# Block-sparse attention and a squared-relu layer on one core: PSUM banks oldest first, later landing times, and score visits of two slots in part of the third batch

## The chip, the cores and the metric

The kernel runs on one core of a Trainium2 chip. The metric is the time of one execution on the device in microseconds (us); a kernel is described by the median of several executions. The profile is of one execution. Its span runs from the first to the last instruction of the program, and the execution's own time is a little longer.

A core has five engines that run side by side, each working through its own instructions in order: TensorE (PE in the profile; its weight loads are listed apart as PEld), VectorE (DVE), ScalarE (ACT), GpSimd (POOL) and SyncE (SP), which here only issues DMAs. Matrix products land in PSUM, an accumulation store of eight banks. ACT and DVE read it from there; POOL works only on SBUF here.

## The reference, cut to what matters

Inputs are q, k and v (4 batches, 8 heads, 768 positions, 64 values), a list of sampled blocks, and two weight matrices. Attention is dense arithmetic under a mask of 32 by 32 blocks, and a two-layer network with a squared relu follows:

```python
scores = scale * np.matmul(q, k.transpose(0, 1, 3, 2))
mask = np.abs(blk_i - blk_j) <= window
mask = mask | (blk_i == 0) | (blk_j == 0) | (blk_i == n_blocks - 1) | (blk_j == n_blocks - 1)
for qb in range(n_blocks):
    for kb in sampled_blocks[qb]:
        mask[qb * block:(qb + 1) * block, kb * block:(kb + 1) * block] = True
scores = np.where(mask, scores, -1000000000.0)
scores = scores - np.max(scores, axis=-1, keepdims=True)
attn = np.exp(scores)
attn = attn / (np.sum(attn, axis=-1, keepdims=True) + 1e-09)
return np.matmul(attn, v).astype(np.float32)
...
x = attn_out.transpose(0, 2, 1, 3).reshape(B * S, H * D)   # 3072 x 512
h = x @ w_in                                               # 512 -> 2048
r = np.maximum(h, 0.0)
g = r * r
return (g @ w_out).astype(np.float32)                      # 2048 -> 512
```

## The kernel before, in words

**Tiling.** Heads are taken in pairs, four pairs to a batch, 16 in all. A *slot* is one piece of attention: a head pair, a tile of queries (128 wide for the first 256 queries of the first batch, 256 wide elsewhere) and two or three chunks of 128 keys. The slots stand in one list, `order`: 40 for the first batch, then 36 for each of the other three. A slot's steps are:

- `scores` (L443): K times Q on TensorE, with the two heads in the two halves of the array's rows, 64 rows each. For the first 256 queries of the first batch the mask is added by a further matmul (L447).
- `exps` (L454): the exponential, on ACT, from PSUM into SBUF (pT).
- `masks` (L461): elsewhere DVE multiplies pT by a mask tile MK of zeros and ones.
- `values` (L483): pT times V on TensorE, with a column of ones that gives the sum; `normalize` (L491, L493) on DVE divides, and the result is transposed into xT, by TensorE in the first batch (L500) and by DMA later (L512).

TensorE does scores in a 64-row mode and nearly everything else in a 128-row mode. The planner charges 0.096 us (`SWITCH`) for a change between them. To change less often, `attend` takes several slots in one *visit*: `GROUPS` says for each batch, and each third of its queries, how many. A 3 stands for all slots of one pair and query tile, which are three.

The dense layers work on tiles of 128, 256 or 384 tokens. `hidden` (L541) makes units of two or four chunks of the 2048 hidden columns, each unit in two or four parts that the planner places one by one; `relu` (L550 on ACT, L552 on DVE) and `square` (L560 on ACT, L562 on POOL) follow, and `output` (L585) accumulates over 16 chunks in bank py. Tokens of one batch pass the dense layers while the next batch is in attention, and the last batch's run alone at the end.

**PSUM.** Two banks serve `po` and `py`. The other six are three tiles X of 1024 columns, two banks each. A slot of scores takes a whole tile (`X2`), as does a unit of hidden columns of a 384-token tile. Transposes, mask tiles and the 512-column hidden units of the first batch take one bank (`X1`). `bank()` chooses: each candidate has a key, the lowest wins.

**Order of the work.** It is computed on the host, before anything runs, by the planner `run_schedule`: it keeps an expected time for each engine and buffer, and each step puts next the task that can start first; ties go by `key` (made uneven by `tie`, from `SEEDS` and `TIES`). The instructions then stand in that order in each engine's queue, held on the chip by semaphores, not by the planner's times. The durations, latencies (`LAT`), `AHEAD` (how much earlier a task of the dense layers must be to go ahead of one of attention with a key under 100), `bias` (a handicap for an engine when a task may go to several), `PACE0` and `PACE` (the earliest time for a batch's scores, by slot), `LEAD` (how long before that the casts of Q and K may start) and `arrive` (when each first-batch input is assumed to have landed) are numbers of the plan alone.

**Loads.** SP issues the first batch's inputs at the start, and ACT two K loads. Later pairs come through `load` on SP, held by `loads_gate`, small DMAs that wait for parts of w_out. POOL issues the weights' DMAs (L417, L420) behind a small copy (L414) that waits for one of the first batch's V loads. Casts (L248 on DVE and POOL, L246 on ACT) and transposes bring Q and K into QK; from the second batch on the transposes are DMAs on SP (L402).

Of the kernel before, what the change touches and what calls it, by code (L numbers as in the profile page):

```python
# [25 lines left out]
def kernel(  # L26
# [21 lines left out]
    HP = H // 2  # L48
# [24 lines left out]


    CB, GATES = 0.4, (6, 7)
    GROUPS = (1, 1, 1), (2, 2, 2), (3, 3, 3), (3, 3, 3)
    QT0, ADDED, ALONE = [(0, 128), (128, 128), (256, 256), (512, 256)], (0, 128), (0, 128)
    MASKED = ((256, 512, 6.5), (512, 768, 8.0), (0, 256, 38.0))
    tasks = []
    LAT = {"PE": 0.23, "DVE": 0.06, "ACT": 0.06, "POOL": 0.08, "SP": 1.4}  # L80
    OVER = {"PE": 0.0, "DVE": 0.08, "ACT": 0.09, "POOL": 0.03, "SP": 0.0}
    SWITCH, SHARE, SLACK = 0.096, 0.85, 0.1
    AHEAD = {"PE": 0.043, "DVE": 0.108, "ACT": 0.176, "POOL": 0.0, "SP": 0.0}
    LEAD = 5.943
    HOLD = 0
    PACE0, PACE, SINGLE, MASK_AT = 39.28, 1.726, 1, 17.0

# [1 line left out]
    class Buf:  # L91
        def __init__(self, pool):
# [2 lines left out]

    TIES = 2.583, 1.777
    SEEDS = (
            621053, 621053, 621053, 162164, 486097, 621053, 621053, 88936, 279485,  # L100
            617998, 621925, 997023, 39474, 741514, 621053, 644142, 104467, 983473,
            256392, 272690, 973551, 604649, 254998, 99264)

    def tie(n):
        x = (n + 1) * 2654435761 & 0xFFFFFFFF ^ SEEDS[n // 64] * 2246822519 & 0xFFFFFFFF
# [18 lines left out]
    def run_schedule(free, bufs, dma_free, mode=128):  # L124
# [12 lines left out]
        def bank(pool, now, gone):  # L137
            n = 2 if pool == "X2" else 1
            best = None
            for c in range(0, 6, n):  # L140
                mine = [cells[i] for i in range(c, c + n)]
                if any(i in gone for i in range(c, c + n)) or any(b and b.holds for b in mine):
                    continue
                r = max([now] + [b.free for b in mine if b])
                o = cells[c ^ 1]
                k_ = (round(r, 4), n == 1 and not (o and o.holds), c)
                if best is None or k_ < best[0]:
                    best = (k_, c, r)
            return best
# [448 lines left out]
    def T_(engs, key, f, *args, **kw):  # L598
        return Task(engs, key, (lambda e: f(*args, e)), **kw)
# [1 line left out]


    arrive = {(0, 1, 0): 3.4, (0, 0, 0): 4.2, (0, 1, CP): 4.55, (1, 0, 0): 5.7, (1, 1, 0): 6.7, (2, 0, 0): 7.2, (2, 1, 0): 8.3, (0, 2, 0): 9.4,
              (3, 0, 0): 9.8, (3, 1, 0): 10.9, (1, 2, 0): 12.4, (2, 2, 0): 13.5, (3, 2, 0): 14.6}
    arrive.update({(u, 0, 2): (15.5, 16.2, 16.8, 17.5)[u] for u in range(HP)})

    KEYS_OF = {P: [tuple(range(CP)), tuple(range(CP, NCH))], QW: [(2 * c, 2 * c + 1) for c in range(CP)]}
    OPEN = [(0, 0), (0, 1), (1, 0), (2, 0), (1, 1), (3, 0), (2, 1), (3, 1)]
# [56 lines left out]
    def attend(group, add):  # L665
        s = min(order.index(a) for a in group)
        bufs = {a: Buf("X2") for a in group}
        area = sum(a[2] * len(a[3]) for a in group) / 512
        deps = [ev[a[0]][1, n] for a in group for n in a[3]]
        deps += [ev[a[0]][0, n] for a in group for n in range(a[1] // P, (a[1] + a[2]) // P)]  # L670
        sc = T_(("PE", (0.44 if add else 0.22) * area), s, scores, group, add, bufs,
                deps=deps + (mr[:1 + (group[-1][1] + group[-1][2] > QW)] if add else []) + sc_all[-1:], get=[bufs[a] for a in group], mode=64,
                after=PACE0 + PACE * (s - N0) * (1.06 - 0.0006 * (s - N0)) if s >= N0 else 0.0, paced=group[0][1] >= QW or s >= N0)
        sc_all.append(sc)
        for i, a in enumerate(group):
            u, q0, w, cs = a
            sc_of[u].append(sc)
            s = order.index(a)
            part = w * len(cs) / 512
            pt = Buf("pT")  # L680
            ex = T_(("ACT", 0.2 + 0.82 * part), s, exps, a, deps=[sc], lead=sc.engs["PE"] * (len(group) - 1 - i) / len(group), get=[pt], put=[bufs[a]])
            if not add:
                ex = T_(("DVE", 0.68), s - 1, masks, a, deps=[ex] + [mk[n, c] for n in cs for c in range(q0, q0 + w, P)], port=True)
            if cs[0] == 0:
                ob[u, q0] = Buf(po_pool(u, q0))
            va = T_(("PE", 0.245 * part), s + 2.023, values, a, deps=[ex] + cv[u] + va_all[-1:] + (kws if po_pool(u, q0) == "y" else []),
                    get=[] if cs[0] else [ob[u, q0]], put=[pt], mode=128)
            va_all.append(va)
            va_of[u].append(va)
            if cs[-1] == NCH - 1:  # L690
                b, a_ = divmod(u, HP)
                by_dma = b > 0
                xqb = Buf("xq")
                nm = T_(("DVE", 0.3 + 0.16 * w / P), s - 9, normalize, u, q0, w, deps=[va], get=[xqb], put=[ob[u, q0]] if by_dma else [])
                kw = {}
                if b not in xb:
                    xb[b] = Buf("xT")
                    kw = dict(get=[xb[b]])
                if by_dma:
                    mu[u, q0] = T_(("SP", 1.22), s - 9, x_transp_dma, u, q0, w, deps=[nm], put=[xqb], dma=0.6, **kw)  # L700
                    continue
                xt = T_(("PE", 0.06 * w / P), s - 9, x_transp, u, q0, w, deps=[nm], put=[xqb], mode=128)
                mu[u, q0] = T_({"DVE": 0.11 + 0.09 * w / P, "ACT": 0.2 + 0.09 * w / P}, s - 9, x_evac, u, q0, w, deps=[xt], put=[ob[u, q0]], **kw)
# [10 lines left out]
    kws = []  # L714
# [28 lines left out]
    for k_, T in enumerate(TILES + [None]):  # L743
        hs = [(T, f) for f in range(0, NF, per_unit(T))] if T else []
        ys = [(TILES[k_ - 1], i, part) for i in range(len(y_tiles(TILES[k_ - 1]))) for part in range(NY)] if k_ else []
        both = [((i + 0.5) / len(hs), 0, x) for i, x in enumerate(hs)]
        both += [((i + 0.5) / len(ys), 1, x) for i, x in enumerate(ys)]
        for _, kind, x in sorted(both, key=lambda z: z[:2]):
            n_key += 1
            t = x[0]  # L750
            b, c0, w = t
            if kind == 0:
                f = x[1]
                need = [mu[b * HP + a, q0] for a in range(HP) for q0, qw in QT[b] if q0 < c0 + w and c0 < q0 + qw]
                w *= per_unit(t)
                wide = w > 512
                hb, rb = Buf("X2" if wide else "X1"), Buf("r")
                last_use = c0 + t[2] == S and f + per_unit(t) == NF
                parts = 4 if wide else 2
                hd = []  # L760
                for part in range(parts):
                    end = part == parts - 1
                    hd.append(T_(("PE", HID[w] / parts), n_key - (0.6 if part else 0.5), hidden, t, f, part, parts, hb,
                                 deps=hd[-1:] or need + [wl[f * NWP // NF], wl[(f + per_unit(t) - 1) * NWP // NF]],
                                 get=[] if part else [hb], put=[xb[b]] if last_use and end else [], mode=128, yields=not part))
                h1 = hd[-1]
                rr = T_(RELU[w], 200, relu, t, f, deps=[h1], get=[rb], put=[hb], bias={"ACT": 0.092})
                n = 1 if wide else per_unit(t)
                for i in range(0, per_unit(t), n):
                    gb = Buf("g")  # L770
                    gbuf[t, f + i + n - 1] = gb
                    sq = T_(SQ[n * t[2]], n_key, square, t, f, i, n, deps=[rr], get=[gb], put=[rb], bias={"ACT": 0.673})
                    sq_of.update({(t, f + i + j): sq for j in range(n)})
            else:
                _, i, part = x
                ts, cs = y_tiles(t)[i]
                n = (cs[1] - cs[0]) / d_model
                fs = range(part * NF // NY, (part + 1) * NF // NY)
                if part == 0:
                    yb = Buf(y_pool(t, i))  # L780
                last_i = i == len(y_tiles(t)) - 1
                yy = T_(("PE", 0.432 * n), n_key, output, t, i, ts, cs, part, yb,
                        deps=[sq_of[t, f] for f in fs] + [wl[NWP + f * NWP // NF] for f in fs] + ([yprev] if part else []),
                        get=[] if part else [yb], put=[gbuf[t, f] for f in fs if (t, f) in gbuf] if last_i else [], mode=128)
                yprev = yy
                if part == NY - 1:
                    sb = Buf("ys")
                    yc = T_({"ACT": 0.22 + 0.365 * n, "DVE": 0.15 + 0.53 * n}, 150, out_copy, t, i, cs, deps=[yy], get=[sb], put=[yb])
                    T_(("SP", 0.55), 0, store, t, i, ts, cs, deps=[yc], put=[sb], late=2.0, dma=0.7)
# [34 lines left out]
```

## Time and profile before

| | |
|---|---|
| median of 5 executions | 277.69 us (276.65 to 277.8) |
| the profiled execution's own time | 277.8 us |
| its span | 276.0 us |
| TensorE busy | 262.0 us (95%), clock 0.999 |
| ACT busy | 224.6 us (81%) |
| DVE busy | 166.6 us (60%) |
| POOL busy | 86.8 us (31%) |
| DMA, mean over the span | 134 GB/s |

A line of a timeline gives the start, the length, the engine, the line of the kernel, the operation, what it writes and reads, and how many instructions are merged; a bracket at its end is the idle time of the engine just before it, and what ended that. A line of the waits gives who waited for whom, the total in us, how many times, and the longest. Matmuls are pipelined: a group's length includes the last one's way through the array, so the cost of one is read from the distance between starts. Some matmul records are missing from the trace; the weight loads are complete.

### The profile page before, as it was taken

What the parts mean: (1) busy time and instruction counts of PE and PEld (TensorE: products, weight loads), DVE (VectorE), ACT (ScalarE), POOL (GpSimd) and SP (SyncE); (2) the same over time, 40 slices, a digit from 0 to 9 for tenths busy, and PEclk for the clock granted to TensorE, in tenths of its full rate; (3) what the DMA queues carried; (4) which work ended last, traced back from release to release, by engine and by line L of the source; (5) the groups of instructions that cost most, each with busy time, mean ns of one, the idle gap of its engine ahead of it and who ended that gap; (6) DMA issues with size and microseconds to landing.
All of it is one profiled execution on the core that took longest, in us unless ns stands there. A gap on an engine that the chain in (4) does not pass through costs nothing.

```text
span 276.0 us, 7322 instructions
## 1 busy us (share of the span) xinstructions
PE 262.0 (95%) x2992; PEld 166.3 (60%) x3032; DVE 166.6 (60%) x339; ACT 224.6 (81%) x294; POOL 86.8 (31%) x110
## 2 busy tenths in 40 slices
PE   8988999889998999999999999999999999999995
PEld 5776665766566565556656556656565666555544
DVE  7886999743877888666856476685665565011010
ACT  3788999958997999999989999899798998646511
POOL 3192327444621126533131251312221112333210
PEclk9999999999999999999999999999999999999999
DMA  6999999999572229765771123442411011011112
GB/s 195 373 214 201 208 221 334 297 287 354 117 216 57 59 40 208 137 216 139 214 219 21 48 63 67 103 72 60 104 57 43 20 57 50 10 40 39 38 68 84
DMA packets 51881, 36.91 MB, mean 134 GB/s; under 512 B 30984, under 2 KB 48904, under 8 KB 51848
## 3 DMA queue, kind: packets, MB, share of 16 engines
q1 hardware_dynamic: 47080, 31.86, 42.2%
q0 software_dynamic: 4224, 4.19, 9.4%
q8 instruction: 23, 0.38, 0.6%
q10 hardware_dynamic: 544, 0.39, 0.5%
q14 instruction: 10, 0.08, 0.1%
HBM read 27.26 MB, written 6.29 MB: 122 GB/s over the span
## 4 chain that ended last, share of the span: by engine, by line
PE 86%; ACT 4%; DVE 4%; issue 3%; DMA 2%; SPq 1%; ACTq 0%; DVEq 0%
PE X L541 30%; PE py L585 27%; PE X L443 12%; PE po L483 12%; DMA ks<-in_k_dram 2%; PE X L585 2%; ACT pT L454 2%; ACT r L550 2%; DVE pT L461 1%; DVE QK L248 1%; SPq L274 1%; PE X L365 1%; PE X L395 1%; PE po L500 0%; DVE MK L373 0%
## 5 line engine op out<-in xcount | busy, mean ns | idle before, releaser
L454 ACT ACTIVATE pT<-X 128x1024 bf16<-128x1024 f32 (+1 forms) x148 | 138.1, 1008 | 8.8 <-PE X L443 6.1
L461 DVE TENSOR_TENSOR pT<-pT,MK 128x1024 bf16<-128x1024 bf16 x132 | 93.4, 728 | 24.2 <-ACT pT L454 23.4
L562 POOL TENSOR_TENSOR g<-r 128x384 bf16<-128x384 f32 (+1 forms) x65 | 59.3, 914 | 151.2 <-ACT r L550 128.6
L541 PE MATMUL X<-xT,w_in_sb 128*128 128x384 bf16 (+2 forms) x640 | 99.8, 294 | 2.9 <-ACT r L550 2.5
L585 PE MATMUL py<-w_out_sb,g 128*128 128x512 bf16 (+1 forms) x328 | 87.6, 374 | 3.4 <-issue 1.9
L541 PEld LDWEIGHTS <-w_in_sb 128*128 128x128 bf16 x640 | 54.4, 97 | 33.1 <-issue 6.7
L550 ACT ACTIVATE r<-X 128x768 f32<-128x768 f32 (+1 forms) x65 | 48.7, 755 | 22.2 <-PE X L541 19.3
L483 PEld LDWEIGHTS <-pT 128*128 128x128 bf16 x1152 | 47.4, 98 | 17.7 <-issue 4.2
L483 PE MATMUL po<-VT,pT 128*128 128x65 bf16 x1152 | 53.3, 193 | 0.1
L585 PEld LDWEIGHTS <-g 128*128 128x128 bf16 x400 | 34.3, 98 | 27.8 <-issue 4.4
L443 PE MATMUL X<-QK 64*128 64x256 bf16 (+1 forms) x624 | 46.6, 263 | 1.9 <-ACT pT L454 1.1
L443 PEld LDWEIGHTS <-QK 64*128 64x128 bf16 x624 | 25.9, 94 | 20.2 <-issue 15.4
L560 ACT ACTIVATE g<-r 128x384 bf16<-128x384 f32 (+1 forms) x55 | 29.8, 542 | 3.0 <-DVE r L552 1.4
L491 DVE RECIPROCAL rs<-po 128x4 f32<-128x4 f32 (+1 forms) x52 | 9.3, 179 | 35.5 <-PE po L483 35.3
L248 DVE COPY ys<-py 128x512 f32<-128x512 f32 x17 | 11.7, 686 | 27.6 <-PE py L585 27.6
L493 DVE TENSOR_TENSOR xq<-po,rs 128x256 bf16<-128x256 f32 (+1 forms) x52 | 21.0, 404 | 1.8
L248 POOL CAST VT<-vs 128x768 bf16<-128x768 f32 x15 | 15.7, 1044 | 19.2 <-issue 11.2
L248 DVE CAST qc<-ks 128x768 bf16<-128x768 f32 (+1 forms) x15 | 11.3, 753 | 0.8 <-DMA ks<-in_k_dram 0.7
L248 DVE CAST qc<-qs 128x768 bf16<-128x768 f32 (+2 forms) x16 | 9.6, 604 | 0.0
L246 ACT COPY ys<-py 128x512 f32<-128x512 f32 (+1 forms) x6 | 3.3, 558 | 5.5 <-PE py L585 5.3
L447 PE MATMUL X<-R,oh 64*128 64x128 bf16 x96 | 6.7, 216 | 0.0
L585 PE MATMUL X<-w_out_sb,g 128*128 128x512 bf16 (+1 forms) x32 | 6.0, 326 | 0.0
(54 smaller groups left out, 76.3 us busy)
## 6 DMA issues: line engine op xcount, KB each, us to landing
vs<-in_v_dram SPq DMA_DIRECT2D x16, 384.0 KB, 6.7
out_dram<-ys SPq DMA_DIRECT2D x23, 256.0 KB, 2.0
ks<-in_k_dram SPq DMA_DIRECT2D x15, 384.0 KB, 5.0
qs<-in_q_dram SPq DMA_DIRECT2D x12, 384.0 KB, 4.0
w_in_sb<-in_moe_w_in_dram POOLq DMA_DIRECT2D x4, 512.0 KB, 9.7
w_out_sb<-in_moe_w_out_dram POOLq DMA_DIRECT2D x4, 512.0 KB, 16.0
qs<-in_q_dram SPq DMA_DIRECT2D x4, 256.0 KB, 7.7
xT<-xq SPq DMA_TRANSPOSE x36, 2.3
```

What stands on the lines that cost most here:

```text
L248: (V if e == "DVE" else G).tensor_copy(out=out, in_=in_)
L443: nc.tensor.matmul(ps[:, h, j * w:(j + 1) * w], QK[i][hs, 1, ksl], QK[i][hs, 0, qsl], start=j == 0, stop=not add, skip_group_check=True)
L454: A.activation(out=pT[:, :, 0:n], in_=stile.pop(a)[:, :, 0:n], func=AF.Exp, scale=scale)
L461: V.tensor_tensor(out=pT, in0=pT, in1=m[:, None].broadcast_to([P, 2, len(cs), w]), op=AOP.mult)
L483: nc.tensor.matmul(po[:, qc, h, :], pT[:, h, j * w + qc * P:j * w + (qc + 1) * P], VT[i][:, h, n, 0:VW], start=(n == 0 and qc == 0 and h = ...
L491: V.reciprocal(out=rs, in_=po[:, :, :, D:VW])
L493: V.tensor_tensor(out=xq, in0=po[:, :, :, 0:D], in1=rs.broadcast_to([P, n, 2, D]), op=AOP.mult)
L541: nc.tensor.matmul(htile[T, f][:, i], w_in_sb[:, kc, (f + i) * P:(f + i + 1) * P], xT[b][:, kc, c0:c0 + w], start=(kc == 0), stop=(kc == K ...
L550: A.activation(out=to, in_=src, func=AF.Relu)
L560: A.activation(out=g, in_=r, func=AF.Square)
L562: (G if e == "POOL" else V).tensor_mul(out=g, in0=r, in1=r)
L585: nc.tensor.matmul(ytile[T, i], gtile[T, f][:, ts * P:(ts + 1) * P], w_out_sb[:, f, cs[0]:cs[1]], start=(f == 0), stop=(f == NF - 1))
```

## The change

It has these parts:

- `bank()`: a bank's place in the choice is set by the time at which it was freed plus 0.8 us, where that is later than the present time, in place of the time at which it was freed. Whether a partner bank is in use, and the number of the bank, still settle ties.
- `arrive`: the V loads of pairs 1, 2 and 3 are assumed to land at 13.4, 14.5 and 15.4 us (12.4, 13.5, 14.6 before), the last queries at 16.1, 16.7, 17.3 and 17.9 (15.5, 16.2, 16.8, 17.5).
- `GROUPS`: the first two thirds of the third batch's queries are visited in twos rather than threes.
- The planner's numbers: the seeds and sizes of the ties, `AHEAD`, `LEAD`, `PACE0`, `PACE`, the place of `values` behind its scores, and ACT's bias for relu and square.

No instruction of the computation is added or taken away.

```diff
-    GROUPS = (1, 1, 1), (2, 2, 2), (3, 3, 3), (3, 3, 3)
+    GROUPS = (1, 1, 1), (2, 2, 2), (2, 2, 3), (3, 3, 3)
...
-    AHEAD = {"PE": 0.043, "DVE": 0.108, "ACT": 0.176, "POOL": 0.0, "SP": 0.0}
-    LEAD = 5.943
+    AHEAD = {"PE": 0.031, "DVE": 0.078, "ACT": 0.219, "POOL": 0.0, "SP": 0.0}
+    LEAD = 9.606
     HOLD = 0
-    PACE0, PACE, SINGLE, MASK_AT = 39.28, 1.726, 1, 17.0
+    PACE0, PACE, SINGLE, MASK_AT = 41.486, 1.677, 1, 17.0
...
-    TIES = 2.583, 1.777
+    TIES = 1.442, 1.763
     SEEDS = (
-            621053, 621053, 621053, 162164, 486097, 621053, 621053, 88936, 279485,
-            617998, 621925, 997023, 39474, 741514, 621053, 644142, 104467, 983473,
-            256392, 272690, 973551, 604649, 254998, 99264)
+            355681, 98427, 98427, 98427, 857545, 98427, 97069, 50148, 911331,
+            98427, 50466, 222927, 270327, 703620, 362781, 613003, 726090, 53435,
+            690252, 701928, 821263, 803756, 192065, 79588)
...
                 r = max([now] + [b.free for b in mine if b])
                 o = cells[c ^ 1]
-                k_ = (round(r, 4), n == 1 and not (o and o.holds), c)
+                old = max([now] + [b.free + 0.8 for b in mine if b])
+                k_ = (round(old, 4), n == 1 and not (o and o.holds), c)
...
-              (3, 0, 0): 9.8, (3, 1, 0): 10.9, (1, 2, 0): 12.4, (2, 2, 0): 13.5, (3, 2, 0): 14.6}
-    arrive.update({(u, 0, 2): (15.5, 16.2, 16.8, 17.5)[u] for u in range(HP)})
+              (3, 0, 0): 9.8, (3, 1, 0): 10.9, (1, 2, 0): 13.4, (2, 2, 0): 14.5, (3, 2, 0): 15.4}
+    arrive.update({(u, 0, 2): (16.1, 16.7, 17.3, 17.9)[u] for u in range(HP)})
...
-            va = T_(("PE", 0.245 * part), s + 2.023, values, a, deps=[ex] + cv[u] + va_all[-1:] + (kws if po_pool(u, q0) == "y" else []),
+            va = T_(("PE", 0.245 * part), s + 3.182, values, a, deps=[ex] + cv[u] + va_all[-1:] + (kws if po_pool(u, q0) == "y" else []),
...
-                rr = T_(RELU[w], 200, relu, t, f, deps=[h1], get=[rb], put=[hb], bias={"ACT": 0.092})
+                rr = T_(RELU[w], 200, relu, t, f, deps=[h1], get=[rb], put=[hb], bias={"ACT": 0.112})
...
-                    sq = T_(SQ[n * t[2]], n_key, square, t, f, i, n, deps=[rr], get=[gb], put=[rb], bias={"ACT": 0.673})
+                    sq = T_(SQ[n * t[2]], n_key, square, t, f, i, n, deps=[rr], get=[gb], put=[rb], bias={"ACT": 0.721})
```

## The prediction

> **What bounds the kernel now.** I read first the page's busy times and slices: TensorE is the only engine near its limit, and the throttle never took its clock.
>
> ```profile
> PE 262.0 (95%) x2992; PEld 166.3 (60%) x3032; DVE 166.6 (60%) x339; ACT 224.6 (81%) x294; POOL 86.8 (31%) x110
> ```
>
> Busy time hides when the idle 14.0 us fall, so next comes busy time by stage (columns: stretch, length, busy time with instructions of PE, weight loads, DVE, ACT, POOL, clock, DMA share, GB/s). The cuts are mine: opening, rest of the first batch's attention, a stretch without score visits, second batch, third, fourth, and what is left of the dense layers.
>
> ```profile
> 0.00:20.00 20.00, 17.39 (x277) 13.06 (x278) 15.90 (x50) 12.93 (x23) 8.70 (x27) 1.00 0.90 265
> 20.00:50.00 30.00, 27.75 (x467) 19.27 (x470) 25.61 (x60) 28.31 (x37) 11.77 (x12) 1.00 1.12 248
> 50.00:63.00 13.00, 11.20 (x148) 9.10 (x147) 6.52 (x13) 9.53 (x17) 5.12 (x5) 1.00 1.17 282
> 63.00:105.00 42.00, 40.53 (x516) 26.40 (x523) 32.31 (x60) 37.77 (x46) 14.56 (x13) 1.00 0.53 135
> 105.00:165.00 60.00, 58.92 (x646) 35.95 (x654) 40.16 (x72) 55.13 (x70) 21.07 (x24) 1.00 0.53 142
> 165.00:232.00 67.00, 65.69 (x712) 40.09 (x726) 42.32 (x81) 60.77 (x75) 14.86 (x18) 1.00 0.28 62
> 232.00:276.00 44.00, 40.54 (x243) 22.47 (x242) 3.81 (x7) 20.17 (x32) 10.75 (x13) 1.00 0.14 50
> ```
>
> PE's idle time is 2.6, 2.3 and 1.8 us in the first 63 us, 1.5 in the second batch, 1.1 and 1.3 in the two after it, 3.5 in the last (nearly all of it the last copy and store, which nothing here touches). Later on PE is full: work added there lengthens the program, and only waits before about 105 us can be taken away. PE's waits, by who ended them:
>
> ```profile
> PE X L541 <- ACT r L550: 2.5, 4, 0.8
> PE py L585 <- issue: 1.9, 12, 0.2
> PE X L443 <- ACT pT L454: 1.1, 2, 1.0
> PE X L365 <- ACT MK L371: 0.4, 1, 0.4
> PE X L443 <- DVE MK L373: 0.4, 1, 0.4
> ```
>
> The "issue" line is mostly missing records (328 and 32 matmuls of L585 shown beside 400 weight loads), not a wait. What a change of banks can reach is 2.5 + 1.1 = 3.6 us: hidden-layer matmuls waiting for a relu, scores waiting for an exponential. The longest of the first kind, in PE's and ACT's order of time:
>
> ```profile
> 52.19 1.49 PE L541 MATMUL X<-xT,w_in_sb 128*128 128x128 bf16 x20
> 54.49 0.60 PE L541 MATMUL X<-xT,w_in_sb 128*128 128x256 bf16 x4 [0.81 <-ACT r L550]
> ...
> 53.86 0.58 ACT L550 ACTIVATE r<-X 128x512 f32<-128x512 f32 x1
> ```
>
> The 20 matmuls are a unit of 16 and the first half (4) of a 256-wide unit; the wait comes before its second half. That half writes a bank which the unit already holds, so it can't be waiting for that bank. It waits for the relu of another unit, which I take to sit in the other bank of the same 1024-column tile X.
>
> **What the skill says.** The Trainium skill, TensorEngine Tiling (Array Packing), section Key Properties: a change of tiling mode drains TensorE. The trace agrees, and prices it below. The skill, Perfetto Trace Analysis, section Optimizing Tensor Performance, Matmuls: "Independent matmul groups should rotate through different PSUM banks so the ACT/DVE evacuation of one overlaps the next group's matmuls". The wait above is a case where that overlap fails.
>
> **The change part by part, on the profiled execution.** Its span is 276.0 us and its time 277.8; the median of the runs is 277.69.
>
> *Third batch, two thirds in visits of two slots.* 24 slots were 8 visits of three (12 matmuls) and become 12 visits of two (8 matmuls): matmuls and exponentials stay, four visits are added, each with two mode changes. Their price, from a visit of two in the second batch:
>
> ```profile
> 104.37 0.38 PE L585 MATMUL py<-w_out_sb,g 128*128 128x512 bf16 x1
> 104.68 0.61 PE L443 MATMUL X<-QK 64*128 64x256 bf16 x8
> 105.23 0.42 PE L483 MATMUL po<-VT,pT 128*128 128x65 bf16 x8
> ```
>
> One output matmul takes 0.216 us start to start (4 took 0.86 in the chain), but 104.68 - 104.37 = 0.31: entering costs 0.095. The 8 score matmuls run two at a time, 4 x 0.108 = 0.43 (0.108 is half of the 0.216 for half the columns), but take 105.23 - 104.68 = 0.55: leaving costs 0.1. Four visits add 4 x 0.195 = +0.8 us. The eight old visits start between 112.6 and 148.5 us, where PE has no idle to hide them, so I count all of it. Below it can go only if new visits fall next to each other; in the trace they stand apart. A visit of two holds two of the three tiles X rather than three, so a hidden unit can keep the third: a possible gain in waiting, but that stretch has almost no waiting to give back.
>
> *Oldest bank first.* The rule ranks a free bank by the time it was freed plus 0.8 us, where that is later than now. The old rule took all banks that are free by now as equal, then the one whose neighbour is in use, then the lowest number. No instruction is added. It reaches the 3.6 us. Against it: among banks freed over 0.8 us ago the neighbour in use still wins, which is just the pairing that the trace shows waiting. I take half: -1.8, with bounds 0 and -3.6.
>
> *Later landings.* Three values loads are assumed 0.8 to 1.0 us later, the last queries 0.4 to 0.6. GpSimd's copy L414, which waits for the third values load, starts at:
>
> ```profile
> 14.22 0.18 POOL L414 COPY held<-vs 1x2 f32<-1x2 f32 x1 [3.59 <-DMA vs<-in_v_dram]
> ```
>
> so that load lands near 14.2: 13.5 was too early, 14.5 is nearer. For the pair before it I have no such row. The order of PE, DVE and ACT between 9 and 17 us is laid out for these times, and behind a late input everything on an in-order engine stands. PE's waits in that stretch are 0.44 at 15.2 us (the L365 line above) and three of 0.22 to 0.24 at 9.4, 10.6 and 15.8 us, behind DVE's casts and copies: 1.1 in all. I take half, -0.6, with bounds -1.1 and, should some inputs now be used too late, +0.6.
>
> *Draws, bias, lead and pace.* New seeds reshuffle ties; relu and square lean a little more away from ACT; values stand 1.2 places later behind scores. Casts of K and Q may start earlier: 39.28 - 5.94 = 33.3 becomes 41.49 - 9.61 = 31.9 us at the second batch's first slot. Their casts, two DMA transposes a pair and the loads queued behind those on SP are the same in number, moved ahead; SP's queue waits longest for w_out to land (26.3 us), which they don't touch. Second-batch scores fall due 2.2 us later, but the first visit there, at 64.2 us, is long past its due time. The last third falls due some 3 us earlier, into a full PE: order, not work. I put 0 here, bounds +1.0 and -1.0 (about one wait of the longest kind).
>
> Sum: +0.8 - 1.8 - 0.6 = -1.6 us: a span of 274.4, and with what lies around it a median of 277.69 - 1.6 = 276.1 us.
>
> **Rivals.** *Two-slot visits bring waits (slower).* The second batch, served in twos, leaves PE idle 1.47 of 42 us (3.5%), the third, in threes, 1.08 of 60 (1.8%). If 40 us of the third take the second's rate, that is +0.7, with the mode changes +1.5: 279.2 us if the first 105 us give nothing. It decides where they give less than 0.7. For it: the added price is certain, the gain is not, and the wait found in mid-unit is of a kind that the new rule doesn't name. Against: that rate is set by one wait of 0.75 us at 86.6, not by the visits.
>
> *Even.* Banks and landings give back just about the mode changes, because a wait removed before 63 us is met again at the next late relu: 277.7, within 0.8.
>
> *The rule changes nothing.* If few banks are ever free for less than 0.8 us when one is picked, the plan keeps its pairs; the mode changes and half the landings remain: +0.8 - 0.6, 277.9. That lies in the even case.
>
> *ACT becomes the bound.* ACT is busy 55.1 of 60 us in the third batch. It gets no more work, so I give this no chance of its own.
>
> **How the numbers follow.** Gains before 105 us outweigh the mode changes: 0.57, with its own range 274.2 to 276.8. Even: 0.16. Slower: 0.27, from 278.5 to about 279.6. About 0.3% (0.8 us) is what a measurement of this kernel tells from no change. The bounds summed would allow 277.69 + 0.8 - 3.6 - 1.1 - 1.0 = 272.8 at best and 277.69 + 0.8 + 0.7 + 0.6 + 1.0 = 280.8 at worst, both needing every term at its end. I keep 273.8 to 278.9: 0.06 lies below, 0.12 above.
>
> **What would show it.** Mode changes: 12 visits of 8 matmuls and then 4 of 12 in the third batch, each costing about 0.2. Banks: X L541 waiting for r L550 under 1.3 us in all; the waits in mid-unit at 53 to 61 us gone. Landings: PE idle before 20 us below 2.6 by about 0.6. The last visit and the start of the score-free end should both come about 1.6 us earlier, and the last 44 us keep their length. I am wrong if the idle time before 105 us, now 8.1 us, is not smaller by more than 0.8, or if the third batch's idle grows past 1.8.

## The result and the profile after

The changed kernel is slower: a median of 278.65 us (43 executions) against 277.6 us (80 executions of the kernel before, among them the five of 277.69 above), ratio 1.0039 with an interval of 1.0027 to 1.005, so +1.1 us (0.7 to 1.4). I had forecast 276.1 us, and the rival that ends slower from 278.5 us. The profiled execution took 278.56 us and its span is 276.7 us, 0.7 more than before.

The busy times of the changed kernel, and its stages with the cuts of the prediction (same columns):

```profile
PE 263.6 (95%) x2994; PEld 164.2 (59%) x3032; DVE 171.9 (62%) x339; ACT 219.3 (79%) x286; POOL 95.0 (34%) x118
```

```profile
0.00:20.00 20.00, 17.05 (x282) 12.25 (x284) 15.59 (x51) 12.67 (x20) 9.66 (x28) 1.00 0.95 273
20.00:50.00 30.00, 27.58 (x462) 19.12 (x461) 26.02 (x59) 28.32 (x39) 9.86 (x10) 1.00 1.13 264
50.00:63.00 13.00, 11.86 (x156) 9.91 (x157) 9.25 (x15) 8.03 (x15) 7.69 (x8) 1.00 1.19 218
63.00:105.00 42.00, 40.16 (x522) 25.89 (x528) 36.20 (x62) 37.20 (x44) 15.75 (x14) 1.00 0.53 139
105.00:165.00 60.00, 59.52 (x635) 34.63 (x643) 41.06 (x70) 53.18 (x68) 26.29 (x30) 1.00 0.58 145
...
```

TensorE's idle time in the first four stages is 2.95, 2.42, 1.14 and 1.84 us, 8.35 in all; before it was 8.13. The forecast needed it to fall by more than 0.8. In the third batch TensorE is all but full: 0.48 us idle, 1.08 before. Both traces lack some 40 of the 3032 matmul records, and their gaps count as idle time, so the two figures are not a gain. The waits of TensorE in the changed kernel:

```profile
PE X L542 <- DVE r L553: 1.5, 3, 0.6
...
PE po L484 <- DVE xq L494: 0.8, 1, 0.8
PE X L396 <- DVE MK L374: 0.7, 2, 0.4
PE X L542 <- ACT r L551: 0.6, 1, 0.6
PE X L444 <- ACT pT L455: 0.5, 1, 0.5
PE X L396 <- DVE qc L249: 0.5, 1, 0.5
PE po L501 <- DVE xq L494: 0.5, 1, 0.5
...
```

The wait of hidden matmuls for ACT's relu fell from 2.5 to 0.6 us, but that for a relu on DVE rose from 0.3 to 1.5: together 2.8 before and 2.1 after. TensorE also waits for DVE's normalised output xq, 0.8 + 0.5 us (none before), and for mask tiles and casts. Two of these in order of time. The first is a mid-unit wait as before the change, the second is new:

```profile
56.89 0.28 PE L501 MATMUL po<-identb,xq 128*128 128x128 bf16 x2
57.80 0.60 PE L542 MATMUL X<-xT,w_in_sb 128*128 128x256 bf16 x4 [0.63 <-ACT r L551]
...
76.72 0.66 PE L484 MATMUL po<-VT,pT 128*128 128x65 bf16 x16 [0.78 <-DVE xq L494]
```

The last score visit starts at 225.37 us (229.11 before), 3.7 us earlier and not 1.6; more of the dense layers is left for the end.

### The profile page after: what moved, and what is told of

The parts are those of the page before. It is cut to its first block, busy times and chain, and to the rows that moved or that the text cites. A ratio compares the mean times of both kernels' runs of the same rounds, so it can differ in the third digit from the quotient of the medians.

```text
span 276.7 us, 7350 instructions
## 1 busy us (share of the span) xinstructions
PE 263.6 (95%) x2994; PEld 164.2 (59%) x3032; DVE 171.9 (62%) x339; ACT 219.3 (79%) x286; POOL 95.0 (34%) x118
## 4 chain that ended last, share of the span: by engine, by line
PE 83%; DVE 7%; ACT 3%; DMA 2%; issue 2%; SPq 1%; DVEq 0%; ACTq 0%
PE X L542 30%; PE py L586 25%; PE po L484 13%; PE X L444 12%; DVE pT L462 3%; ACT pT L455 2%; DMA ks<-in_k_dram 2%; PE X L586 2%; DVE QK L249 1%; DVE r L553 1%; DVE xq L494 1%; SPq L275 1%; PE X L396 1%; DVE MK L374 1%; ACT MK L372 1%
## 5 line engine op out<-in xcount | busy, mean ns | idle before, releaser
L563 POOL TENSOR_TENSOR g<-r 128x384 bf16<-128x384 f32 (+1 forms) x73 | 68.4, 942 | 148.4 <-ACT r L551 125.8
L462 DVE TENSOR_TENSOR pT<-pT,MK 128x1024 bf16<-128x1024 bf16 x132 | 100.8, 789 | 15.9 <-ACT pT L455 15.8
L542 PE MATMUL X<-xT,w_in_sb 128*128 128x384 bf16 (+2 forms) x640 | 101.2, 294 | 2.6 <-DVE r L553 1.5
L551 ACT ACTIVATE r<-X 128x768 f32<-128x768 f32 (+1 forms) x62 | 46.8, 759 | 29.0 <-PE X L542 28.5
L444 PEld LDWEIGHTS <-QK 64*128 64x128 bf16 x624 | 25.1, 94 | 22.3 <-issue 17.9
L249 DVE COPY ys<-py 128x512 f32<-128x512 f32 x13 | 8.9, 688 | 31.5 <-PE py L586 31.4
L561 ACT ACTIVATE g<-r 128x384 bf16<-128x384 f32 (+1 forms) x47 | 25.3, 540 | 2.4 <-DVE r L553 1.2
L249 POOL CAST VT<-vs 128x768 bf16<-128x768 f32 x15 | 14.4, 962 | 15.5 <-issue 9.2
L553 DVE TENSOR_SCALAR r<-X 128x512 f32<-128x512 f32 (+1 forms) x10 | 7.4, 742 | 4.8 <-PE X L542 4.2
L247 ACT COPY ys<-py 128x512 f32<-128x512 f32 (+1 forms) x10 | 5.8, 576 | 5.5 <-PE py L586 5.3
```

Source lines behind the costliest of these rows:

```text
L249: (V if e == "DVE" else G).tensor_copy(out=out, in_=in_)
L444: nc.tensor.matmul(ps[:, h, j * w:(j + 1) * w], QK[i][hs, 1, ksl], QK[i][hs, 0, qsl], start=j == 0, stop=not add, skip_group_check=True)
L462: V.tensor_tensor(out=pT, in0=pT, in1=m[:, None].broadcast_to([P, 2, len(cs), w]), op=AOP.mult)
L542: nc.tensor.matmul(htile[T, f][:, i], w_in_sb[:, kc, (f + i) * P:(f + i + 1) * P], xT[b][:, kc, c0:c0 + w], start=(kc == 0), stop=(kc == K ...
L551: A.activation(out=to, in_=src, func=AF.Relu)
L553: V.tensor_scalar(out=to, in0=src, scalar1=0.0, scalar2=None, op0=AOP.max)
```

## The experiments

### Is a mode change paid in full?

The kernel before, with each of the eight three-slot visits cut after the plan is made. `late` is a task for the third slot; it is put behind the TensorE task that follows the first two:

```diff
+            v = getattr(t, "visit", None)
+            if v and 2 * HP <= v[0][0][0] < 3 * HP and v[0][0][1] < 2 * QW:
+                slots, add, bufs = v
...
+                t.fn = lambda e, s=slots, b=bufs: scores(s[:2], False, b, e)
...
+                late.fn = lambda e, s=slots, b=bufs: scores(s[2:], False, b, e)
```

> The kernel before, instruction for instruction, but for the eight three-slot visits in the first two thirds of the third batch: each is cut into two slots and one, with TensorE's next task between them. That adds 8 visits, 16 mode changes. Theory (each mode change is paid in full, 0.095 to 0.1 us, because TensorE has no idle there): 16 x 0.097 = +1.6 us, a ratio of 1.0056. Rival (the changes hide in waits, or finer visits feed ACT better): within 0.3% of before.

Measured: 278.99 us against 277.12, ratio 1.0077 (1.0048 to 1.0106), +2.1 us (1.3 to 2.9). The span is 277.8 us, +1.8. For each of the 16 mode changes that is 0.13 us by the ratio and 0.11 by the span. The trace shows one visit as two:

```profile
112.80 0.61 PE L468 MATMUL X<-QK 64*128 64x256 bf16 x8
113.34 0.60 PE L610 MATMUL py<-w_out_sb,g 128*128 128x512 bf16 x2
113.88 0.39 PE L468 MATMUL X<-QK 64*128 64x256 bf16 x4
```

Two output matmuls of 0.216 us fill 0.54 us between the two visits, so entering cost 0.11. TensorE's waits are those of before (2.5 us for relu again). The theory stands: finer visits hide nothing there and gain nothing. The weight loads show 148 mode changes before, 164 with the visits cut and 156 in the changed kernel; its 8 further ones cost 0.8 us at the 0.097 of the trace, and 1.1 us at half of what the cut visits cost.

### What are the waits in mid-unit?

The order of every engine is kept. When the plan is done, and before anything is emitted, banks are given out anew by a search that keeps the 200 best ways at each step. A way costs something where TensorE writes a tile X less than 1.2 us (`NEED`) after the planned end of a read of the same tile, in either bank. In the diff, `mine` are the buffers of X that a TensorE task writes, and `r` has the last read of each tile:

```diff
+                    for b in mine:
+                        late = NEED - (t.began - r[c.index(id(b)) // 2])
+                        at += max(0.0, late) ** 2
...
             ready.remove(t)
+            t.began = at
+            emitted.append((t, e))
+        settle(emitted)
+        for t, e in emitted:
             t.fn(e)
```

> The kernel before with every engine's order kept; only the banks of the shared tiles are given out anew, so that no tile X is written soon after any bank of it was read. Theory (the waits in mid-unit come from a relu that reads the other bank of the same tile, since the waits are kept for the whole tile): the four waits of hidden matmuls for relu at 54.5, 59.8, 61.1 and 86.6 us, 2.5 us in all, go, and the kernel is 1.5 to 2.5 us faster, ratio 0.991 to 0.995. Rival (the relu is late because ACT is behind, and TensorE meets the same lateness at its next task): the same waits in other rows, ratio within 0.3% of 1.

Measured: 274.19 us against 277.12, ratio 0.9911 (0.988 to 0.9943), 2.5 us faster (1.6 to 3.3); span 271.9. It beats both kernels. First all the waits of TensorE that the view of waits lists for it, then, in order of time, the place where the kernel before stood still at 54.5 us:

```profile
PE X L348 <- DVE bm L338: 1.2, 1, 1.2
PE X L483 <- DVE r L592: 0.6, 1, 0.6
PE X L405 <- ACT MK L411: 0.3, 1, 0.3
PE X L405 <- DVE QK L288: 0.2, 1, 0.2
PE X L483 <- DVE QK L288: 0.2, 1, 0.2
PE X L483 <- issue: 0.2, 1, 0.2
```

```profile
50.86 1.93 PE L581 MATMUL X<-xT,w_in_sb 128*128 128x128 bf16 x24
52.62 0.27 PE L540 MATMUL po<-identb,xq 128*128 128x128 bf16 x2
52.73 1.04 PE L581 MATMUL X<-xT,w_in_sb 128*128 128x256 bf16 x8
```

No hidden matmul waits for a relu any more; the 1.0 us of scores for exponentials is gone too. One visit of scores now waits 0.6 us for a relu. Only bank numbers differ, so the waits come from the banks. The plan of the kernel before says which banks. Counted from 0 to 5, two to a tile, the matmuls at 54.5 us write bank 3 and the relu that they wait for reads bank 2; at 59.8 us it is 1 and 0, at 61.1 us 0 and 1, at 86.6 us 3 and 2. Each time it is the other bank of the same tile. So the semaphores guard the tile X as a whole, a write to one of its banks waits for a relu that reads the other, and the planner books single banks and doesn't see it. The changed kernel's four waits for relus are of the same kind. The sentence on rotating through PSUM banks in the Trainium skill (Perfetto Trace Analysis, Optimizing Tensor Performance, Matmuls) agrees with this run, but the rotation has to be by the tile that the semaphores guard.

### What is the new rule worth?

The rule alone in the kernel before, and taken out of the changed one:

```diff
-                k_ = (round(r, 4), n == 1 and not (o and o.holds), c)
+                old = max([now] + [b.free + 0.8 for b in mine if b])
+                k_ = (round(old, 4), n == 1 and not (o and o.holds), c)
```

> The kernel before with the rule of the oldest bank alone, the plan made anew; its order departs from that of before only after some 42 us. Theory (the rule leaves the pairing of two units in one tile): the waits of hidden matmuls for relu in mid-unit stay near 2.5 us, ratio 0.997 to 1.003. Rival (as I forecast: half of 3.6 us of waits goes): ratio about 0.9935.

> The changed kernel with the old rule for banks, all else as changed; its order departs from the changed kernel's only after some 42 us. Theory (the rule is worth little): within 0.3% of the changed kernel, so 1.001 to 1.007 of the kernel before. Rival (the rule did bring its 1.8 us and something else ate it): slower than the changed kernel by 1.8 us, about 1.0105 of the kernel before.

Measured: alone 277.18 us against 277.12, ratio 1.0 (0.9982 to 1.0018). Taken out, 281.25 us, ratio 1.0151 (1.0123 to 1.018), 2.6 us above the changed kernel's median. My theory holds for the first and falls for the second. With the rule alone the waits for relu are even a little longer:

```profile
PE X L542 <- ACT r L551: 3.0, 5, 0.9
```

So the rule is worth 0 in one plan and some 2.6 us in another. Only part of the 2.6 shows as waits for relus, 2.9 us with the rule taken out against 2.1. Either it works through the banks or through the order that it leads the planner to. To tell these apart, both kernels of this pair and the changed kernel had their banks given out anew, as above, with their orders kept:

> The changed kernel with every engine's order kept and only the banks given out anew, so that no tile X is written soon after any bank of it was read. Theory (waits of the whole tile are in the changed kernel too, and its extra visits stay paid): the hidden matmuls' waits for relu and exponential at 50.0, 57.8, 61.0 and 87.6 us go, 2.0 us, the one at 31.3 us may stay; about 276.5 us, ratio 0.994 to 0.999 of before, and still 1.5 to 3 us slower than the kernel before with its banks apart. Rival (the changed order's late normalisation by DVE takes the place of these waits): no faster than the changed kernel, ratio 1.003 or more.

> The changed kernel with the old rule for banks, its order kept and its banks then given out anew, apart as before. It shares with the changed kernel everything but the order that the old rule leads to. Theory (the rule acts through the banks: with the banks given out by another hand, its 2.6 us are gone): within 0.4% of the changed kernel with banks apart, ratio 0.997 to 1.005 of before. Rival (the rule acts through the order that it leads the planner to): slower than the changed kernel with banks apart by 1.5 us or more, ratio over 1.006.

> The kernel before with the new rule alone, its order kept and its banks then given out anew, apart as before. Theory (with the banks given out by another hand, the order that the rule leads to is worth nothing either way): within 0.4% of the kernel before with banks apart, ratio 0.987 to 0.995 of before. Rival (the order matters): ratio outside of that.

| order of | banks of its planner | banks apart | ratio of the latter to before |
|---|---|---|---|
| before | 277.6 us | 274.19 us | 0.9911 (0.988 to 0.9943) |
| before, rule alone | 277.18 us | 273.82 us | 0.9858 (0.9813 to 0.9903) |
| changed | 278.65 us | 277.74 us | 1.0007 (0.9992 to 1.0021) |
| changed, rule out | 281.25 us | 277.53 us | 1.0001 (0.9982 to 1.002) |

Within each pair the rule's effect vanishes (the intervals overlap): as far as these runs tell, it acts through the banks alone. In the second row the ratio 0.9858 lies just below the 0.987 that my theory allowed. The two medians of that job give 273.82 / 277.18 = 0.988, and both profiled spans with banks apart in this pair are 271.9 us, so I don't read an effect of the order into it. Between the pairs stands 1% of the time (1.0007 against 0.9911, 2.7 us; 3.5 us in the medians) that this new choice of banks doesn't touch. My expectation for the changed kernel with banks apart, 276.5 us, was missed, and so was its rival's, 1.003 or more. Three of its four hidden waits went (57.8, 61.0 and 87.6 us), 0.9 us of the median with them; what stays, below the 1.2 us ahead of the first matmul, begins with this:

```profile
PE po L524 <- DVE xq L534: 0.8, 1, 0.8
PE X L436 <- DVE qc L289: 0.5, 2, 0.4
PE X L484 <- ACT pT L495: 0.5, 1, 0.5
PE X L582 <- DVE r L593: 0.5, 1, 0.5
PE po L541 <- DVE xq L534: 0.5, 1, 0.5
PE X L436 <- DVE MK L414: 0.3, 1, 0.3
PE X L406 <- DVE QK L289: 0.3, 1, 0.3
...
```

Six of these seven are waits for DVE, 2.9 us; beside 0.6 + 0.2 + 0.2 in the kernel before with banks apart. These two traces have all 3032 matmul records, so their idle times can be compared. The stages before 105 us, first of the kernel before, then of the changed one, both with banks apart:

```profile
0.00:20.00 20.00, 17.88 (x290) 13.38 (x291) 16.08 (x52) 13.52 (x24) 9.88 (x28) 1.00 0.96 275
20.00:50.00 30.00, 28.94 (x488) 20.09 (x488) 25.99 (x60) 28.89 (x38) 10.72 (x11) 1.00 1.14 266
50.00:63.00 13.00, 13.00 (x149) 10.01 (x147) 6.78 (x13) 10.89 (x19) 6.16 (x6) 1.00 1.15 284
63.00:105.00 42.00, 41.66 (x544) 26.57 (x543) 35.26 (x65) 38.72 (x48) 16.22 (x16) 1.00 0.49 127
```

```profile
0.00:20.00 20.00, 17.46 (x274) 12.54 (x276) 15.88 (x50) 12.48 (x20) 9.20 (x27) 1.00 0.94 269
20.00:50.00 30.00, 27.77 (x463) 19.21 (x463) 24.28 (x57) 27.25 (x37) 9.60 (x10) 1.00 1.14 263
50.00:63.00 13.00, 12.30 (x164) 10.24 (x164) 10.61 (x17) 9.30 (x17) 9.12 (x9) 1.00 1.00 206
63.00:105.00 42.00, 41.14 (x539) 26.33 (x537) 37.10 (x63) 37.81 (x45) 15.86 (x15) 1.00 0.55 146
```

TensorE is idle for 3.52 and 6.33 us. The 2.8 us between them and the 0.8 of the mode changes make 3.6 of the 4.0 us between the two spans (271.9 and 275.9). So the worse order shows where attention and the dense layers share the engines early on, mostly as waits for DVE.

### Does the lean of relu and square make DVE late?

```diff
-                rr = T_(RELU[w], 200, relu, t, f, deps=[h1], get=[rb], put=[hb], bias={"ACT": 0.112})
+                rr = T_(RELU[w], 200, relu, t, f, deps=[h1], get=[rb], put=[hb], bias={"ACT": 0.092})
...
-                    sq = T_(SQ[n * t[2]], n_key, square, t, f, i, n, deps=[rr], get=[gb], put=[rb], bias={"ACT": 0.721})
+                    sq = T_(SQ[n * t[2]], n_key, square, t, f, i, n, deps=[rr], get=[gb], put=[rb], bias={"ACT": 0.673})
```

> The changed kernel with the old lean of relu and square (0.092 and 0.673); TensorE's order stays the same, ACT, DVE and GpSimd share relus and squares otherwise from about 51 us on. Theory (the lean to GpSimd slows DVE's mask products beside it, and so makes the new waits for DVE's normalisation): PE po waiting for xq at 76.7 us (0.8) shrinks, time falls by 0.5 to 1 us from the changed kernel, ratio 1.000 to 1.002 of before. Rival (that wait comes from the casts on GpSimd at that place, not from squares): within 0.3% of the changed kernel, ratio 1.002 to 1.006.

Measured: 278.54 us, ratio 1.0053 (1.0037 to 1.0069) to before, the changed kernel's 1.0039 within error. That is in the rival's range, and the theory's gain did not come. But the run puts little back: GpSimd does 72 squares in it, 73 in the changed kernel and 65 in the kernel before. So it clears the lean as such, not the squares on GpSimd. DVE, then GpSimd, ahead of the wait at 77 us:

```profile
72.44 3.99 DVE L462 TENSOR_TENSOR pT<-pT,MK 128x1024 bf16<-128x1024 bf16 x3
76.35 0.17 DVE L492 RECIPROCAL rs<-po 128x4 f32<-128x4 f32 x1
76.55 0.42 DVE L494 TENSOR_TENSOR xq<-po,rs 128x256 bf16<-128x256 f32 x1
```

```profile
72.20 1.21 POOL L563 TENSOR_TENSOR g<-r 128x512 bf16<-128x512 f32 x1 [1.38 <-ACT r L551]
73.37 1.28 POOL L249 CAST qc<-qs 128x768 bf16<-128x768 f32 x1
74.60 1.28 POOL L249 CAST VT<-vs 128x768 bf16<-128x768 f32 x1
```

The three mask products take 1.53, 1.3 and 1.3 us beside a square and two casts on GpSimd; the 80 of this trace that no instruction of GpSimd overlaps take 0.68 to 0.69. Not every one beside GpSimd is slow (0.72 at 81.3 us, beside a square). The normalisation in DVE's queue behind them is late, and the bank po with it. That GpSimd's work is at fault is what the rows suggest, and whether by its casts or its squares they don't tell: the casts on GpSimd number 20 before and after, the squares are eight more. No kernel with either moved was tried.

### What do the landing times and the draws carry?

The later landings alone; then the draws of the ties switched off (`TIES` = 0, 0), and each of landings and rule on top of that:

```diff
-              (3, 0, 0): 9.8, (3, 1, 0): 10.9, (1, 2, 0): 12.4, (2, 2, 0): 13.5, (3, 2, 0): 14.6}
-    arrive.update({(u, 0, 2): (15.5, 16.2, 16.8, 17.5)[u] for u in range(HP)})
+              (3, 0, 0): 9.8, (3, 1, 0): 10.9, (1, 2, 0): 13.4, (2, 2, 0): 14.5, (3, 2, 0): 15.4}
+    arrive.update({(u, 0, 2): (16.1, 16.7, 17.3, 17.9)[u] for u in range(HP)})
```

> The kernel before with the later landings alone, the plan made anew with the old draws. Theory (the draws of ties fit one plan only, so any early edit loses them): several us slower, 3 to 12, ratio 1.01 to 1.04, with more idle TensorE well after the opening. Rival (as I forecast: landings act only in the opening): 0.6 us faster, ratio about 0.998.

> The kernel before with the draws of the ties switched off (both sizes of TIES at 0), so that equal tasks go by their plain keys. Theory (the draws fit one plan only, and that fit is what the later landings alone lost): about as slow as the later landings alone, ratio 1.02 to 1.045. Rival (the loss came from the landing times themselves): within 1% of before.

> The draws switched off, and the later landings. Theory (without a fit to lose, landings are worth under 1 us either way): within 0.4% of the kernel without draws. Rival (later landings hurt in themselves): slower than the kernel without draws by over 1%.

> The draws switched off, and the rule of the oldest bank. Theory (the rule's worth is what the plan makes of it, since it keeps the pairing in one tile): within 0.5% of the kernel without draws, with hidden matmuls still waiting for relu and scores for exponentials, in all within 1.5 us. Rival (the rule takes half of the waits for banks in any plan): faster than the kernel without draws by 0.6% or more.

| kernel | median | ratio to before |
|---|---|---|
| later landings alone | 288.01 us | 1.0384 (1.0347 to 1.0422) |
| no draws | 286.49 us | 1.0343 (1.0296 to 1.0389) |
| no draws, later landings | 284.94 us | 1.0286 (1.0245 to 1.0328) |
| no draws, rule | 285.33 us | 1.0313 (1.0263 to 1.0363) |

Seven assumed landing times moved by at most 1 us cost 10.6 us, and not in the opening (2.46 us idle there, 2.61 before). These two stages are of the kernel with the later landings alone:

```profile
20.00:50.00 30.00, 25.20 (x454) 18.39 (x454) 25.76 (x65) 28.89 (x38) 3.24 (x5) 1.00 1.13 258
63.00:105.00 42.00, 39.44 (x523) 26.11 (x522) 33.05 (x60) 37.97 (x46) 15.38 (x14) 1.00 0.44 124
```

TensorE's idle time there is 4.8 and 2.6 us (2.25 and 1.5 before), so 3.6 of the loss; where the rest arises was not traced. Without any draws the kernel is slow by nearly as much, and then the same landings do no harm: 1.5 us faster in the medians, with intervals that overlap (0.5%, where I had allowed 0.4). So the theory on the draws holds for this edit: they fit the plan closely, and an edit of inputs due at 12 to 18 us loses what they bring. Edits that change the order only later lost nothing: the rule alone (from some 42 us on) and the lean in the changed kernel (from about 51 us on). The rule without draws is 1.2 us faster in the medians, again with overlapping intervals, and relus are still waited for (2.6 us, 3.2 without it). The medians leave room for both parts to be worth about 1 us when there is no fit to lose.

## Why the prediction was wrong

The table of orders and banks splits the change. Each measured span runs from the ratios within a job to the medians above, which were not all taken together; the ratios' own intervals are not added. The third term is what the two others leave:

| term | forecast | measured | from |
|---|---|---|---|
| mode changes of four further visits | +0.8 | +0.8 to +1.1 | 8 at 0.097 (trace) to 0.13 (cut visits) |
| banks | -1.8 | -1.6 to -2.5 | bank waits cost the kernel before 0.89% (2.5) or 277.6 - 274.2 = 3.4, the changed one 278.65 - 277.74 = 0.9 |
| landings, draws, lean, pace | -0.6 + 0 | +1.6 to +2.8 | orders with banks apart differ by 0.96% (2.7) or 277.74 - 274.19 = 3.55; less the mode changes |
| sum | -1.6 | +1.1 | |

- **Visits.** Right, size included. The third batch had nothing to give back, as said. The slower rival's own mechanism, waits that come with visits of two, did not appear: the third batch's TensorE idle did not grow (0.48 us). The rival got its sign from elsewhere.
- **Banks.** The place of the waits and their cause were right (the other bank of the same tile, now shown), and so was the doubt that the rule doesn't name that cause. The size was about right too, but by luck: in the kernel before, the rule takes nothing off, while in the changed order it takes 2.6 us off. The sign that I named, under 1.3 us of waits for ACT's relu, came out at 0.6 in the letter only, since relus on DVE took part of these waits over; the waits in mid-unit at 53 to 61 us are not gone (57.8 us).
- **Landings, and "I put 0 here, bounds +1.0 and -1.0".** This is the step that failed, and it turned the sign: forecast at -0.6 + 0, it measured +1.6 to +2.8. I priced the landings by the waits in the opening, and the new draws, lead, pace and lean by one long wait either way. But the draws carry some 9 us of this kernel's time (no draws: 1.0343), and an early edit with the old draws loses all of it. The change edits the plan early and brings new draws, and what counts is how well the two together do on the chip. They do about 2 us worse, as idle TensorE before 105 us. A bound for that term has to come from what the fit is worth, not from the size of one wait. No profile of the kernel before shows that size, so the honest range was wider.
- **Opening.** Forecast 0.6 less idle before 20 us; measured 0.3 more (2.61 to 2.95): waits of 0.51, 0.22, 0.38 and 0.39 us at 9.3, 10.5, 13.3 and 16.6 us stand where 0.24, 0.22, 0.44 and 0.22 stood.
- **ACT as the bound.** Right to give it no chance: ACT is less busy than before (219.3 us).

Open: which of the plan's numbers makes the new order worse. It shows as waits for DVE, and putting the lean of relu and square back makes no difference that shows. GpSimd's squares and casts beside DVE's mask products fit the rows; neither was moved. The lead, the pace and the place of values were not put back one at a time.

## What to carry to other kernels

When an order comes from a planner whose random ties are fitted to it, a diff of its inputs is not a sum of parts: its worth is that of the new fit, and a part that acts early, tried alone, mostly measures the fit that was lost. Keep the order and vary one thing after it (banks, cuts of visits); such runs gave the clean answers here. And compare what the planner books with what the semaphores guard: banks were booked, whole tiles were guarded, and giving the banks out by tile gained 2.5 us with no instruction added or moved.

## What the runs showed of the hardware

- The price of a change between the 64-row and the 128-row mode was about 0.1 us each way, read from starts before the change (0.095 and 0.1) and with the visits cut (0.11 and 0.11). Sixteen more of them lengthened the span by 1.8 us.
- A mask product of DVE (128 x 1024, bf16, two inputs) took 0.68 to 0.69 us with GpSimd idle (93 of the 132 before, 78 after), and up to 1.3 us with a cast and 1.53 us with a square and a cast on GpSimd beside it (after, 72 to 76 us). Over the first 105 us the same 56 products kept DVE busy 41.0 us before and 45.3 us after, with GpSimd busy 40.2 and 43.0 us. I had not counted this at all.
